# A new hand-written instruction order ahead of an expert loop, and row scalings moved to the end of the loop's first iteration

## The chip, the cores and the metric

One Trainium2 chip, one of its cores. A core has five engines that each run their own queue in order: PE (matmul; weight loads are listed as PEld), DVE (VectorE), ACT (ScalarE), POOL (GpSimd) and SP (SyncE, which here only issues DMAs). They wait for each other through semaphores alone. The metric is the device time in microseconds (us), the median of several executions.

## What is computed

The program is an attention step in both directions, and behind it a mixture of experts whose routing is balanced in eight rounds. The reference, cut to what matters:

```
# x: (8, 8, 512, 64)  batch, head, token, channel;  state: (8, 8, 32, 64)
scores = x @ state^T / 8 ;  a  = softmax(scores) ;  xread = a  @ state
scores2= state @ x^T / 8 ;  a2 = softmax(scores2);  sread = a2 @ x
X = concat([xread, sread], axis=2) -> (4352, 512)      # 8 x (512 + 32) rows

P = exp(X @ w_gate - max)                              # (4352, 8)
for _ in range(8):                                     # rows, then columns
    P /= P.sum(1) + 1e-9 ;  P /= P.sum(0) + 1e-9 ;  P *= N / E
out = sum over e of  P[:, e] * (relu(X @ w1[e]) @ w2[e])   # w1: 512x1024, w2: 1024x512
```

## The kernel before, in words

The 4352 rows are kept in nine blocks: eight of 512 rows, one for each batch (x's reads), and a ninth of 256 rows (the state's reads). `acc`, the output in fp32, stays in SBUF throughout.

**Ahead of the loop** lies everything up to the routing weights, interleaved with expert 0, so that PE has matmuls while the small work goes on. For each batch b (0 to 7) and half q of its heads: x is loaded by POOL's DMA queue (line 476, two halves a batch), turned either by PE (line 586, batches 0 and 1) or by a DMA transpose on SP's queue (line 599, into `xT`), scored against the state (line 613, one matmul group "S" for each half, numbered 0 to 15), brought through both softmaxes on DVE, ACT and POOL, and for the state's side turned by another DMA transpose on SP's queue (line 752, into `ETs`) for the matmuls that read x (line 775, "R"). Expert 0 needs for each block a projection "V" of w1 through the state (line 901), eight hidden matmul pairs "H" (line 928) with a relu each on ACT or DVE (lines 427, 429), and eight half sums "Y" of four matmuls (line 966). The balancing, on DVE, has eight rounds with one column sum on PE each (line 876). At the end expert 1's first block is begun.

**The order** of all this is written out by hand, as the table PLAN: 768 entries, each a number and an engine (P PE, V DVE, A ACT, G POOL, S SP's DMA queue, H nothing on the chip). An entry is one operation, one to sixty-four instructions. Each engine runs its entries in the table's order; semaphores wait for data and for buffers. PSUM buffers are taken in the table's order from a ring of six banks, so an entry that takes a bank waits until the entries that read the bank's previous content have run. The score banks (one pair) are handed on in the same way. x has five buffers, `xT` four. IDLE lists entries ahead of which PE gets so many dummy transposes.

Entries that are spoken of below:

| entries | what they are |
|---|---|
| 8, 9; 11, 12; 14, 15; 17, 18 | loads of x, first and second half, of batch 0; 1; 2; 3 |
| 24; 26; 29, 30 | loads of x: batch 5 second half; batch 6 first half; batch 7 |
| 51, 52; 53, 54 | loads of expert 0's w1 (two column halves) and w2 (two row halves) |
| 130, 131; 161; 192; 254 | DMA transposes of x: batch 2 both halves; batches 3, 4, 6 first half |
| 76, 91; 159; 190 | DMA transposes of the softmax of score groups 0, 1; 5; 7 |
| 132, 146, 177, 194 | score groups S4, S5, S7, S8 on PE |
| 315, 319, 321 | the matmuls that read x for batches 0, 2, 3 (R1, R5, R7) |
| 436, 470; 441; 479 | V's second half for blocks 0 and 1; first H of block 0; an early H of block 1 |
| 429; 430 to 432 | the last column sum on PE; DVE's three steps behind it |

**The loop** runs over the other experts e and blocks bi, 63 iterations (i). An iteration has seven parts k = 0 to 6. In each, `layer2` issues one of seven matrix products of eight matmuls on PE (line 341) into the banks A, E and Bseed, which DVE adds into `acc` with the routing weight (line 355), and `layer1` issues hidden matmuls of the next block (line 261) whose relu ACT does (line 284, `Hm`); after the fourth and eighth relu DVE makes four sums of them (lines 290 to 293). Two products that use the same bank wait for DVE's addition in between. While e is 1, the next block's four row tiles of `acc` have to be scaled by expert 0's routing weight first (`weigh`: line 303 on ACT, line 305 on DVE or POOL). In iteration 0 no projection falls due, so the parts in which the next block's scalings were issued are 0, 0, 1 and 2, on ACT, each ahead of the relus of its part.

Of the kernel before, what the change touches and what calls it, by code (L numbers as in the profile page):

```python
# [13 lines left out]
AF = mybir.ActivationFunctionType  # L14
EPS = 1e-9
PLAN = """
6G 0S 1S 2V 7H 44V 3A 33V 32A 34A 8G 56P 36P 35V 55H 37V 10H 45V 57A 42P 58V 9G 38P 40P 43A 59P 4S 39A 41V 5V
46V 62P 50H 51G 61A 71V 63P 60A 52G 64V 11G 72V 73A 78P 65V 12G 467P 433P 66A 79V 13H 14G 15G 53G 16H 80V 77P
47P 67V 468A 86V 68V 469A 434A 81A 470P 435A 48A 87V 93P 436P 471A 49A 92H 472A 69P 96P 82V 95V 88A 83V 94V
70V 437A 84P 99P 85V 89V 438A 107A 501P 74V 441P 75G 98V 439P 97V 54G 502A 453P 503A 442A 454A 445P 19H 129H  # L20
440A 100V 17G 443P 108V 101V 449P 447P 504P 102V 446A 114P 444A 451P 103A 109V 90V 450A 461P 336P 110A 115V
448V 116V 464P 130S 122A 354V 505A 506A 104V 160H 111V 132P 117G 452A 140V 458P 455P 118A 123V 462P 456P 459P
141V 18G 105G 337V 119V 76S 112G 106V 142A 465P 124V 133V 143V 134V 120G 91S 463A 125A 144G 131S 121V 146P
466V 113S 126V 457A 477P 135G 460A 479P 478A 147V 161S 154V 475P 487P 148V 136A 20G 155V 480A 21G 156A 145S
483P 137V 149G 473P 162S 485P 481P 163P 476A 488A 474A 150A 484V 315P 489P 486A 316A 191H 482V 495P 138G 127G
171V 164V 498P 128S 172V 22H 165V 173A 192S 166G 535P 167A 151V 177P 496P 152G 537A 497A 23G 222H 490P 139V
185V 499P 174V 186V 157V 158G 153V 187A 536V 509P 491A 317P 500A 168V 178V 318V 569P 179V 538P 510A 175G 169V
194P 539A 540A 202V 25H 570A 159S 571A 180G 195V 24G 492P 196V 517P 27G 197G 193S 493P 511P 519P 176S 181A
521P 203V 182V 513P 494A 188V 204A 507P 518A 520V 515P 512A 26G 514V 170V 508A 208P 198A 522A 216V 183G 209V
319P 184V 523P 516A 205V 526P 217V 199V 223S 524P 320A 210V 527P 218A 189G 200V 224S 547P 532P 225P 549P 219V  # L30
548A 211G 528V 529P 533P 525A 28H 233V 226V 234V 227V 530P 212A 29G 534A 543P 550V 213V 541P 551P 206V 545P
190S 542V 235A 214G 236V 531A 555P 553P 546V 544A 603P 207S 239P 552A 321P 253H 228G 240V 247V 556A 254S 554A
560P 255S 241V 248V 605A 220G 340P 604A 201V 563P 322A 229A 221S 561P 572P 242G 237G 249A 230V 256P 562A 250V
574A 231G 215V 341A 573A 564P 243A 557P 264V 257V 342P 558P 565A 265V 581P 266A 244V 31G 238S 258V 343V 577P
559A 637P 582A 578A 270P 566P 245V 338P 638A 284H 278V 567P 575P 259V 579P 271V 279V 639A 285S 251G 232V 272V
30G 273G 260A 261V 583P 339A 568A 589P 580V 280A 576A 587P 267V 323P 584A 606P 590A 588A 287P 246V 286S 344P
585P 324A 274A 607A 295V 608A 252S 275V 591P 586A 346P 296V 262V 288V 600P 615P 592P 281V 268G 297A 593A 601P
289V 263V 345V 602A 640P 301P 276G 616V 641A 269S 347V 642A 325P 290G 298V 326A 309V 282G 623P 597P 302V 299V
594P 291A 598P 310V 613P 303V 277V 617P 311A 283S 312V 313V 304G 300S 292V 614V 305A 293G 624A 306V 294V 595P
611P 619P 599A 348P 307G 308V 596A 618A 609P 331H 327P 314S 612A 349A 329P 620A 332G 621P 328V 610A 350P 330V  # L40
352P 351V 631P 334G 622A 651P 353V 652A 355V 356P 357V 632P 358P 625P 633A 359V 360A 727H 653P 626P 361V 362V
627A 335G 628P 363V 364V 365V 634P 366P 629P 367V 635P 655P 643P 368V 369V 654A 370V 630A 649P 636A 371V 645P
372V 656A 647P 657P 644A 373V 374V 375P 650V 737P 728H 376V 377V 333G 378V 646A 648A 658A 379V 380V 381V 738A
382V 671P 672A 383V 729V 662P 735G 665P 673A 739A 663P 730G 664A 666P 384P 674P 385V 386V 387V 740P 667A 659P
676A 388V 668P 675A 389V 679P 390V 660P 669P 741A 687P 391V 677P 680A 742A 392V 743H 670A 661V 393P 689P 748P
731G 755P 394V 678A 395V 396V 688A 397V 685P 690A 683P 756A 749A 686A 398V 759P 399V 691P 684A 400V 401V 681P
746P 757P 402P 682V 758V 760A 732V 403V 404V 405V 744P 745V 733G 406V 692A 407V 750P 747A 751A 753P 707P 705P
408V 409V 706A 693P 708A 410V 702P 699P 752V 754A 703P 411P 696P 412V 700P 694P 734G 695A 413V 414V 704V 697P
415V 711P 701A 709P 416V 417V 418V 419V 715P 420P 719P 698V 421V 712A 422V 423V 713P 716A 424V 425V 710A 714A
717P 426V 720A 724P 721P 718A 427V 428V 761V 725P 722P 429P 726A 430V 723A 762P 763A 431V 765P 432V 764A 766V  # L50
736G 767A
""".split()
ENGINES = {"P": "PE", "V": "DVE", "A": "ACT", "G": "POOL", "D": "DMA", "S": "SPQ", "H": "HOST"}
IDLE = {56: 50, 63: 3, 78: 3, 93: 8}
NT_ = 2
NE = 5
ETX = 0
# [13 lines left out]
PATV = (0, 0, 1, 3, 2, 2, 0)  # L71
# [37 lines left out]
def issue(ops, idle):  # L109
    for step in PLAN:  # L110
        op = ops[int(step[:-1])]
        assert all(d.end for d in op.after) and ENGINES[step[-1]] in op.on
        for slot in op.takes:
            slot.ring.taken.append(slot)
            slot.tile = slot.make()
        idle(op.takes[0].tile if op.takes else None, IDLE.get(int(step[:-1]), 0))
        op.emit(ENGINES[step[-1]])
# [5 lines left out]
def kernel(  # L123
# [19 lines left out]
    NTB = N // 128  # L143
# [11 lines left out]
    blocks = [(b * S, S) for b in range(B)] + [(NX, B * Ns)]  # L155
# [10 lines left out]
    def bank(shape, dtype, name, tag="bank"):  # L166
        return pools[tag].tile(shape, dtype, name=name, tag=tag)
# [26 lines left out]
    def load_w(e):  # L194

        w1h = mw.tile([128, NKC, F], FP16, name="w1h", tag="w1h")
        w2h = mw.tile([128, NFB, Dm], FP16, name="w2h", tag="w2h")
        w16[e] = (w1h, w2h)
        for g in range(2):
            nc.gpsimd.dma_start(out=w1h[:, ds(2 * g, 2), :], in_=w1r[e, :, ds(2 * g, 2), :])  # L200
        for g in range(2):
            nc.gpsimd.dma_start(out=w2h[:, ds(NJ * g, NJ), :], in_=w2r[e, :, ds(NJ * g, NJ), :])
        for _ in range(10):
            yield
        T = tpool[0].tile([128, 4, NJ, DH], FP16, name="T", tag="T")
        tsum[e] = T
        b11, b12 = w2h[:, :NJ, :DH], w2h[:, :NJ, DH:]
        b21, b22 = w2h[:, NJ:, :DH], w2h[:, NJ:, DH:]
        for i, (p, q) in enumerate(((b12, b11), (b22, T[:, 0]), (b22, b12), (b21, T[:, 1]))):
            for g in range(2):  # L210
                jj = ds(g * (NJ // 2), NJ // 2)
                nc.vector.tensor_sub(T[:, i, jj], p[:, jj], q[:, jj])
                yield
# [873 lines left out]
    for i, (e, bi) in enumerate(work):  # L1087
        if bi == 1 and e + 1 < E:
            wload.append(load_w(e + 1))
        if (e, bi) == final:  # L1090
            layer2_last()
            break
        v, pat = iter(()), PATS if bi == B else PATN if bi == B - 1 else PAT0
        soon = work[:i + (3 if bi == B - 1 else 2)]
        need = sum(b < B for _, b in soon) * (F // 512)
        if halves and all_halves - len(halves) < need:
            v, pat = project(halves[:SESSION], i), PATV
            del halves[:SESSION]
        if i:
            next(v, None)  # L1100
        if not i:
            seeds += [bank([128, 2, DH], FP32, "Bseed", "B%d" % k) for k in range(2)]
        l2 = layer2(e, bi, i)
        l1 = iter(())
        if i + 1 < len(work) and work[i + 1] not in hid:
            l1 = layer1(*work[i + 1], None if i else seeds[0].rearrange("p c d -> p (c d)"))
        if not i:
            next(l2)
            next(l1)
        for k in range(7):  # L1110
            next(l2)
            step(k)
            if k == 0:
                next(v, None)
                next(v, None)
            if late:
                late.pop()()
            for m in range(4) if e == 1 and bi < B else ():
                lead = pat is PATV and m == 0
                if k == ((0, 4, 5, 6) if pat is PATV else (0, 0, 1, 2))[m] and blocks[bi + 1][0] // 128 + m < NTB:  # L1120
                    weigh(blocks[bi + 1][0] // 128 + m, "DVE" if lead else "ACT")
            for _ in range(pat[k]):
                next(l1, None)
                step(k)
        for part in (l1, l2):
            for _ in part:
                pass
        if bi == len(blocks) - 3:
            for _ in (x for w in wload for x in w):
                pass  # L1130
            wload.clear()
# [30 lines left out]
```

## Time and profile before

| what | value |
|---|---|
| time before, median of 3 runs | 748.18 us (747.88 to 749.77) |
| the profiled execution's own time | 748.45 us |
| its span, first to last instruction | 746.7 us |
| PE / DVE / ACT / POOL busy | 99% / 82% / 69% / 11% of the span |
| first H of block 0 starts (PE, line 928) | 19.1 us |
| last column sum of the balancing (PE, line 876) | 130.5 us |
| the loop's first product (PE, line 341) | 131.2 us |

The profiled execution took 1.75 us more than its span, and 0.27 us more than the median. The span divides at 131.2 us: what lies ahead is the table's, what lies behind is the loop's.

### The profile page before, as it was taken

The numbers are of one execution on the slowest core, as the hardware profiler recorded it, in microseconds if no ns is written. First come the engines' busy times: TensorE is split into PE (matmuls) and PEld (weight loads), VectorE is DVE, ScalarE is ACT, GpSimd is POOL, SyncE is SP. The second block draws the span as 40 slices with busy tenths as digits, with TensorE's granted clock in tenths as the row PEclk, the third lists the DMA queues.
The fourth block names the chain that finished last, engine by engine and source line by source line (L and its number), as shares of the span: only waits on it lengthen the run. The fifth ranks groups of instructions, "written<-read, shape, count | busy, mean of one in ns | idle before, by whom it ended". The sixth has DMA issues, their size and how long they took to land.

```text
span 746.7 us, 16258 instructions
## 1 busy us (share of the span) xinstructions
PE 736.4 (99%) x6579; PEld 505.4 (68%) x6579; DVE 611.2 (82%) x1517; ACT 513.6 (69%) x1002; POOL 81.5 (11%) x97
## 2 busy tenths in 40 slices
PE   7999999999999999999999999999999999999997
PEld 6444545676777667776777767777777767776676
DVE  5989788788888788788888888887887888887885
ACT  6878764898876766767666666667666676667662
POOL 4775530200010000100000000100001000000000
PEclk9999999999999999999999999999999999999999
DMA  9997540600041000600005000330006000012233
GB/s 178 175 159 92 86 79 1 114 1 2 1 85 29 2 1 1 113 2 1 1 16 99 1 1 2 66 48 1 2 1 113 1 2 1 1 39 94 97 113 142
DMA packets 51371, 36.71 MB, mean 49 GB/s; under 512 B 25312, under 2 KB 44000, under 8 KB 51296
## 3 DMA queue, kind: packets, MB, share of 16 engines
q0 software_dynamic: 22272, 20.97, 18.3%
q1 hardware_dynamic: 27840, 14.31, 8.0%
q8 instruction: 51, 0.84, 0.4%
q10 hardware_dynamic: 1184, 0.39, 0.2%
q14 instruction: 24, 0.20, 0.1%
HBM read 42.48 MB, written 8.91 MB: 69 GB/s over the span
## 4 chain that ended last, share of the span: by engine, by line
PE 93%; DMA 2%; ACT 2%; POOL 1%; DVE 1%; issue 1%; SPq 0%; POOLq 0%; ACTq 0%
PE hps L261 28%; PE Bseed L341 20%; PE A L341 14%; PE E L341 14%; PE yps L966 6%; PE hps L928 4%; PE v_ps L241 4%; DMA x_nat<-in_x_dram 1%; DMA xT<-x_nat 1%; PE v_ps L901 1%; PE su_ps L775 0%; PE y L320 0%; ACT acc L303 0%; ACT hT L427 0%; POOL x_nat L476 0%
## 5 line engine op out<-in xcount | busy, mean ns | idle before, releaser
L284 ACT ACTIVATE Hm<-hps 128x512 f16<-128x512 f32 (+1 forms) x495 | 264.6, 576 | 130.7 <-PE hps L261 128.9
L341 PEld LDWEIGHTS <-Hm 128*128 128x128 f16 x1888 | 181.7, 98 | 72.0 <-issue 16.3
L261 PE MATMUL hps<-aT,V 128*128 128x512 f16 x878 | 230.1, 379 | 0.0
L355 DVE SCALAR_TENSOR_TENSOR acc<-Bseed,Pmat,acc 128x256 f32<-128x256 f32 x354 | 155.0, 478 | 9.3 <-PE Bseed L341 6.4
L341 PEld LDWEIGHTS <-sm 128*128 128x128 f16 x1416 | 138.3, 98 | 34.5 <-issue 0.3
L341 PE MATMUL Bseed<-T,Hm 128*128 128x256 f16 x944 | 123.3, 273 | 0.7 <-DVE acc L355 0.7
L341 PE MATMUL A<-w2h,Hm 128*128 128x256 f16 x944 | 123.7, 273 | 0.0
L261 PEld LDWEIGHTS <-V 128*128 128x128 f16 x880 | 86.1, 98 | 50.7 <-ACT V L421 0.2
L355 DVE SCALAR_TENSOR_TENSOR acc<-E,Pmat,acc 128x256 f32<-128x256 f32 x236 | 103.2, 477 | 12.1 <-PE E L341 12.0
L290 DVE TENSOR_TENSOR sm<-Hm 128x512 f16<-128x512 f16 (+1 forms) x122 | 50.3, 412 | 61.1 <-ACT Hm L284 61.1
L249 ACT CAST V<-v_ps 128x512 f16<-128x512 f32 x144 | 74.2, 610 | 0.0
L355 DVE SCALAR_TENSOR_TENSOR acc<-A,Pmat,acc 128x256 f32<-128x256 f32 x118 | 51.9, 480 | 17.2 <-PE A L341 17.1
L966 PE MATMUL yps<-w2h,hT 128*128 128x512 f16 x272 | 64.0, 379 | 0.3 <-ACT hT L427 0.3
L341 PE MATMUL E<-T,sm 128*128 128x256 f16 x472 | 61.7, 273 | 0.1
L341 PE MATMUL E<-w2h,sm 128*128 128x256 f16 x472 | 61.7, 273 | 0.0
L341 PE MATMUL Bseed<-T,sm 128*128 128x256 f16 x472 | 61.6, 272 | 0.0
L365 ACT COPY Bseed<-A 128x512 f32<-128x512 f32 (+1 forms) x62 | 34.1, 550 | 37.6 <-PE A L341 35.1
L291 DVE TENSOR_TENSOR Hm<-Hm 128x512 f16<-128x512 f16 (+1 forms) x122 | 50.2, 412 | 4.2
L293 DVE TENSOR_TENSOR sm<-Hm,sm 128x512 f16<-128x512 f16 (+1 forms) x122 | 50.2, 412 | 4.2
L200 POOL DMA_DIRECT2D w1h<-in_moe_w_dram x12 | 8.6, 717 | 397.0 <-PE hps L261 396.6
L292 DVE TENSOR_TENSOR sm<-sm,Hm 128x512 f16<-128x512 f16 (+1 forms) x122 | 49.4, 405 | 0.0
L966 PEld LDWEIGHTS <-hT 128*128 128x128 f16 x272 | 25.2, 98 | 29.4 <-issue 1.6
(133 smaller groups left out, 621.2 us busy)
## 6 DMA issues: line engine op xcount, KB each, us to landing
out_dram<-acc SPq DMA_DIRECT2D x33, 256.0 KB, 2.6
w1h<-in_moe_w_dram POOLq DMA_DIRECT2D x16, 512.0 KB, 7.0
w2h<-in_moe_w_dram POOLq DMA_DIRECT2D x16, 512.0 KB, 7.5
x_nat<-in_x_dram POOLq DMA_DIRECT2D x16, 256.0 KB, 5.9
st_st<-in_state_dram SPq DMA_DIRECT2D x1, 256.0 KB, 3.9
st_st<-in_state_dram ACTq DMA_DIRECT2D x1, 256.0 KB, 4.5
ETs<-E SPq DMA_TRANSPOSE x16, 3.5
xT<-x_nat SPq DMA_TRANSPOSE x12, 4.3
```

The lines of the kernel that those rows point to most:

```text
L241: nc.tensor.matmul(ps[q][ds(j * Ns, Ns), :], stT[ds(r, 64), bi, q, ds((j ^ q) * Ns, Ns)], w1h[ds(r, 64), 2 * q + j // 2, cols], tile_posit ...
L249: nc.scalar.copy(out=dst, in_=src)
L261: nc.tensor.matmul(out, lhs, rhs, start=(k == 0), stop=(k == len(terms) - 1))
L284: nc.scalar.activation(out=Hm[:, i, j, :tn], in_=hps[:, :tn], func=AF.Relu)
L290: nc.vector.tensor_add(s1, a21, a22)
L291: nc.vector.tensor_sub(a21, a11, a21)
L292: nc.vector.tensor_sub(s2, s1, a11)
L293: nc.vector.tensor_sub(s4, a12, s2)
L341: nc.tensor.matmul(dst[:, c], lhs(j, c), rhs[:, j], start=first and c == 0 and j == 0, stop=(j == NJ - 1), skip_group_check=True)
L355: nc.vector.scalar_tensor_tensor(out=dst, in0=src[:, c], scalar=p[:, k], in1=dst, op0=ALU.mult, op1=ALU.add)
L365: nc.scalar.copy(out=Bb[:, :nk], in_=A[:, :nk])
L966: nc.tensor.matmul(yps.tile, hT[fb].tile[:, ds(tk * 128, 128)], w2h[:, fb, :], start=(fb == 0), stop=(fb == NFB - 1))
```

## The change

The table is replaced by another order of the same 768 entries, some of them on another engine: DVE has 248 entries where it had 241, ACT 186 where it had 185, POOL 58 where it had 66, PE and SP as many as before. IDLE names other entries: 3 dummies ahead of entry 62 and 12 ahead of 436, in place of 3 ahead of 63 and 8 ahead of 93. In the loop, iteration 0 issues the next block's four scalings in its parts 3, 4, 5 and 6, still on ACT and still ahead of the part's relus; the other iterations keep their parts. The diff, with the table cut:

```diff
--- before.py
+++ after.py
@@ -14,44 +14,43 @@
 PLAN = """
-6G 0S 1S 2V 7H 44V 3A 33V 32A 34A 8G 56P 36P 35V 55H 37V 10H 45V 57A 42P 58V 9G 38P 40P 43A 59P 4S 39A 41V 5V
-46V 62P 50H 51G 61A 71V 63P 60A 52G 64V 11G 72V 73A 78P 65V 12G 467P 433P 66A 79V 13H 14G 15G 53G 16H 80V 77P
-47P 67V 468A 86V 68V 469A 434A 81A 470P 435A 48A 87V 93P 436P 471A 49A 92H 472A 69P 96P 82V 95V 88A 83V 94V
-70V 437A 84P 99P 85V 89V 438A 107A 501P 74V 441P 75G 98V 439P 97V 54G 502A 453P 503A 442A 454A 445P 19H 129H
-440A 100V 17G 443P 108V 101V 449P 447P 504P 102V 446A 114P 444A 451P 103A 109V 90V 450A 461P 336P 110A 115V
-448V 116V 464P 130S 122A 354V 505A 506A 104V 160H 111V 132P 117G 452A 140V 458P 455P 118A 123V 462P 456P 459P
-141V 18G 105G 337V 119V 76S 112G 106V 142A 465P 124V 133V 143V 134V 120G 91S 463A 125A 144G 131S 121V 146P
...
-415V 711P 701A 709P 416V 417V 418V 419V 715P 420P 719P 698V 421V 712A 422V 423V 713P 716A 424V 425V 710A 714A
-717P 426V 720A 724P 721P 718A 427V 428V 761V 725P 722P 429P 726A 430V 723A 762P 763A 431V 765P 432V 764A 766V
-736G 767A
+6G 0S 1S 2V 7H 44V 3A 33V 32A 34A 8G 56P 36P 35V 55H 37V 10H 45V 57A 42P 58V 9G 38P 43A 39V 40P 46A 41A 4S 59P
+61A 5V 62P 60A 71V 63P 50H 78P 51G 64V 13H 72V 11G 467P 65V 79V 433P 73A 52G 80V 12G 66A 77P 468A 435A 67V 14G
+53G 47P 54G 86V 49V 434A 469A 81A 436P 87V 470P 68V 129H 48V 88A 437A 69P 16H 438A 471A 472A 93P 82V 96P 83V
+92H 70A 94V 84P 501P 98A 95V 99P 85V 100V 441P 89V 97A 107A 503A 445P 101V 502V 442V 439P 15G 446A 443P 114P
+115V 102G 444A 451P 130S 17G 108V 447P 109V 453P 440A 160H 103A 449P 116V 122A 90V 19H 18G 74V 123V 448A 452A
+131S 161S 110A 104V 117G 461P 454A 111V 450A 105G 112G 455P 75V 458P 118A 124V 504P 132P 462P 506A 140V 133V
+119V 141V 463A 125A 459P 336P 134V 120G 106V 142A 121V 505A 143V 456P 337V 464P 457A 146P 465P 76S 460A 135G
...
+167A 496P 186V 491V 168V 222H 187A 191H 178V 500A 159S 317P 153V 497A 188V 192S 319P 569P 179V 320A 169G 180G
...
+27G 176S 219V 527P 205V 226V 524P 543P 234V 227V 254S 531A 534V 212A 206G 547P 554A 528V 213V 548V 235A 228G
...
+545P 220G 201V 525A 229A 544A 549P 546A 541P 214G 555P 284H 542V 342P 550A 556A 572P 230V 190S 574A 603P 239P
...
+247V 248V 343A 573A 231G 321P 604A 240V 551P 241V 249A 552V 605V 560P 236V 557P 256P 340P 250V 561P 338P 341V
...
+749V 403V 729V 404V 405V 730V 756A 406V 717P 759P 407V 709P 753P 696P 408V 409V 718A 702P 410V 760A 731V 699P
+411P 710A 700P 412V 693P 701A 703P 697P 413V 754A 414V 705P 415V 416V 417V 418V 694P 735G 419V 698A 420P 695A
+704V 707P 761V 711P 744P 706A 708A 719P 712A 750P 421V 422V 713P 736G 715P 423V 424V 425V 426V 427V 745A 720A
+714A 724P 716A 428V 751V 721P 752V 725P 429P 726A 722P 430V 762P 431V 432V 723A 732V 764V 765P 763A 766A 767A
 """.split()
-IDLE = {56: 50, 63: 3, 78: 3, 93: 8}
+IDLE = {56: 50, 62: 3, 78: 3, 436: 12}
@@ -1116,8 +1115,8 @@
             if late:
                 late.pop()()
             for m in range(4) if e == 1 and bi < B else ():
-                lead = pat is PATV and m == 0
-                if k == ((0, 4, 5, 6) if pat is PATV else (0, 0, 1, 2))[m] and blocks[bi + 1][0] // 128 + m < NTB:
+                lead = i and pat is PATV and m == 0
+                if k == ((3, 4, 5, 6) if not i else (0, 4, 5, 6) if pat is PATV else (0, 0, 1, 2))[m] and blocks[bi + 1][0] // 128 + m < NTB:
                     weigh(blocks[bi + 1][0] // 128 + m, "DVE" if lead else "ACT")
             for _ in range(pat[k]):
                 next(l1, None)
```

POOL's queue begins 8 9 51 **52 11** 12 14 **15 53** 75 **54** 17 18 before, and 8 9 51 **11 52** 12 14 **53 54 15** 102 17 18 after (75 and 102 are arithmetic on POOL that waits for DVE). SP's queue begins 130 76 91 131 113 161 145 162 before and 130 131 161 76 91 162 113 128 145 159 192 after; later it has 224 176 254 190 where it had 176 223 224 190 207 254.

More of the change, by code (lines that the diff above doesn't have):

```diff
@@ L22 @@
-448V 116V 464P 130S 122A 354V 505A 506A 104V 160H 111V 132P 117G 452A 140V 458P 455P 118A 123V 462P 456P 459P
-141V 18G 105G 337V 119V 76S 112G 106V 142A 465P 124V 133V 143V 134V 120G 91S 463A 125A 144G 131S 121V 146P
-466V 113S 126V 457A 477P 135G 460A 479P 478A 147V 161S 154V 475P 487P 148V 136A 20G 155V 480A 21G 156A 145S
-483P 137V 149G 473P 162S 485P 481P 163P 476A 488A 474A 150A 484V 315P 489P 486A 316A 191H 482V 495P 138G 127G
-171V 164V 498P 128S 172V 22H 165V 173A 192S 166G 535P 167A 151V 177P 496P 152G 537A 497A 23G 222H 490P 139V
@@ L27 @@
[L27 to L46, printed above, removed]
@@ L47 @@
-746P 757P 402P 682V 758V 760A 732V 403V 404V 405V 744P 745V 733G 406V 692A 407V 750P 747A 751A 753P 707P 705P
-408V 409V 706A 693P 708A 410V 702P 699P 752V 754A 703P 411P 696P 412V 700P 694P 734G 695A 413V 414V 704V 697P
-415V 711P 701A 709P 416V 417V 418V 419V 715P 420P 719P 698V 421V 712A 422V 423V 713P 716A 424V 425V 710A 714A
-717P 426V 720A 724P 721P 718A 427V 428V 761V 725P 722P 429P 726A 430V 723A 762P 763A 431V 765P 432V 764A 766V
-736G 767A
+6G 0S 1S 2V 7H 44V 3A 33V 32A 34A 8G 56P 36P 35V 55H 37V 10H 45V 57A 42P 58V 9G 38P 43A 39V 40P 46A 41A 4S 59P
@@ new lines @@
+119V 141V 463A 125A 459P 336P 134V 120G 106V 142A 121V 505A 143V 456P 337V 464P 457A 146P 465P 76S 460A 135G
+479P 20G 475P 126V 136A 91S 473P 480A 147V 487P 477P 466A 154V 148V 483P 144V 149G 474A 162S 155V 476V 156A
+481P 113S 485P 137V 482V 21G 127V 478A 315P 128S 138V 157V 488A 535P 484A 163P 145S 498P 150A 489P 536A 171V
+164V 316A 172V 486A 22H 165V 158G 495P 538P 173A 151V 166G 177P 490P 139V 539A 499P 540A 537V 185V 23G 152G
+167A 496P 186V 491V 168V 222H 187A 191H 178V 500A 159S 317P 153V 497A 188V 192S 319P 569P 179V 320A 169G 180G
@@ new lines @@
+31G 28H 194P 492P 511P 202V 24G 318A 571A 195V 509P 29G 193S 513P 174V 493P 570A 203V 223S 25H 512A 517P 196V
+181A 510A 519P 182V 494A 204A 514A 521P 197G 224S 507P 183V 508A 518V 170V 30G 198A 26G 520A 515P 208P 216V
+253H 529P 522A 532P 217V 523P 175V 209V 199V 210V 184V 189V 526P 218A 516A 225P 233V 200G 533P 211V 530P 553P
+27G 176S 219V 527P 205V 226V 524P 543P 234V 227V 254S 531A 534V 212A 206G 547P 554A 528V 213V 548V 235A 228G
+545P 220G 201V 525A 229A 544A 549P 546A 541P 214G 555P 284H 542V 342P 550A 556A 572P 230V 190S 574A 603P 239P
@@ new lines @@
+247V 248V 343A 573A 231G 321P 604A 240V 551P 241V 249A 552V 605V 560P 236V 557P 256P 340P 250V 561P 338P 341V
+215V 257V 322A 558P 237V 258V 285S 563P 559V 242G 243A 264V 566P 221S 562A 255S 259G 564P 232V 579P 265V 260A
+261V 244V 266A 567P 267V 339A 251V 637P 580A 270P 286S 344P 245G 565A 262G 639V 568A 575P 278V 246V 581P 331H
+638A 345V 207S 577P 576A 589P 587P 268G 271V 582A 585P 279V 583P 578A 272V 590A 588V 252S 346P 273G 323P 280A
+586A 606P 281V 324A 287P 584V 600P 347A 591P 274A 601P 607A 275V 295V 288V 296V 238S 608A 335G 297A 282G 609P
@@ new lines @@
+592P 602A 640P 301P 276V 289V 325P 642A 593A 290G 298V 309V 594P 597P 310V 610A 302V 299G 595P 291A 311A 303V
+641A 277V 283S 613P 304G 312V 263V 326A 313V 305A 292V 596A 598P 354V 306V 619P 307V 599A 620A 623P 617P 308V
+293G 611P 334G 269S 614A 348P 294V 624A 615P 621P 618A 300S 327P 314S 349V 616A 329P 612A 350P 328V 330A 631P
+351A 622V 352P 353V 355V 632P 633A 356P 357V 625P 358P 634P 359V 360A 628P 361V 362V 727H 647P 363V 635P 333G
+364V 626P 636A 365V 366P 367V 368V 627A 369V 370V 629P 728H 655P 651P 648A 332G 371V 645P 630A 656A 653P 372V
@@ new lines @@
+649P 657P 373V 374V 652A 654A 643P 646A 650A 375P 644A 658V 737P 738A 376V 671P 377V 665P 378V 662P 379V 673A
+380V 381V 666P 739A 663P 382V 383V 733V 384P 385V 386V 672A 740P 734V 667A 664A 674P 741A 675A 387V 668P 388V
+659P 389V 742A 743H 390V 391V 676A 392V 669P 679P 670A 660P 393P 680V 394V 395V 757P 661A 677P 685P 396V 746P
+686A 758V 397V 678A 689P 747A 398V 399V 683P 684A 691P 681P 690A 682A 687P 400V 748P 401V 688A 402P 692V 755P
+749V 403V 729V 404V 405V 730V 756A 406V 717P 759P 407V 709P 753P 696P 408V 409V 718A 702P 410V 760A 731V 699P
```

## The prediction

> **What bounds the kernel now.** I read the page first, then PE by windows, then PE's list of waits, then the chain of work that ended last.
>
> ```profile
> span 746.7 us, 16258 instructions
> ...
> PE 736.4 (99%) x6579; PEld 505.4 (68%) x6579; DVE 611.2 (82%) x1517; ACT 513.6 (69%) x1002; POOL 81.5 (11%) x97
> ```
>
> PE is busy 99% of the span, so a reordering can win back only PE's idle time and what hides inside "busy" (slow clock, late starts). The windows show where that is (columns: busy us and count for each engine, PE's granted clock, DMA share, GB/s):
>
> ```profile
> 10.00:20.00 10.00, 7.61 (x167) 4.57 (x165) 8.98 (x23) 7.94 (x20) 0.82 (x1) 0.83 1.34 199
> 20.00:30.00 10.00, 10.00 (x75) 4.34 (x74) 9.43 (x25) 9.45 (x21) 6.68 (x9) 1.00 1.35 188
> 30.00:40.00 10.00, 9.14 (x98) 4.00 (x96) 8.62 (x20) 7.47 (x17) 8.77 (x10) 1.00 1.21 169
> ...
> 140.00:150.00 10.00, 9.28 (x89) 6.29 (x88) 8.11 (x21) 7.38 (x14) 0.00 (x0) 1.00 0.75 126
> ```
>
> PE misses 2.4 us between 10 and 20, 0.9 between 30 and 40, 0.7 behind 140, and almost nothing elsewhere. Who ends those waits:
>
> ```profile
> PE xT_ps L586 <- DMA x_nat<-in_x_dram: 1.3, 2, 0.7
> PE Bseed L341 <- DVE acc L355: 0.7, 1, 0.7
> PE G_ps L528 <- ACT V L421: 0.7, 1, 0.7
> PE psB L613 <- DMA xT<-x_nat: 0.5, 1, 0.5
> ```
>
> Loads and DMA transposes end the early ones; the one behind 140 is DVE's. For the table I use one measure, PE's **lag**: an entry's start minus PE's issue time for all entries listed ahead of it (from the starts: hidden pair 0.43 us, half sum 0.865, projection or score 0.225, R 0.62, turn of x 0.5). A reordering that makes PE wait less has a smaller lag at the loop. Before, the lag is 12.7 us at 441 (starts 19.14), 13.0 at 132 (25.31), 13.2 at score S6, 14.45 at 177 (39.59), 14.6 at S9, 15.0 at S14, 15.6 at S15 (80.15) and 16.5 at the loop. Much of the slow growth is a change of matmul shape (309 ns where 216 is usual), which no order removes.
>
> **The change part by part.** Times below are places in the profiled execution; a minus is a gain.
>
> *(a) Start, to the first H.* The loads land at 10.7 (51), 13.7 (52), 15.4 (11), 16.7 (12): one after another, an x half in 1.3 to 1.7 us, a w half in 2.6 to 2.95. With 11 ahead of 52, 11 lands near 12.3 and 52 near 15.2. PE now waits at 436 for 52, where it waited for 11 at 15.43. The groups behind the wait are nearly the same ones, but x's turn need not wait any more. Then ACT decides: its evictions from 437 on start at 15.65 and follow each 0.48 us (steps 20.28, 20.77, 21.27 in its timeline), so 441 has its inputs at 18.3 to 18.8 in place of 19.14, and 454 and 450, which free 504's bank and feed the second half sums, end at 24.8 and 25.3. 132 then starts near 25.1 with 13.0 us of work ahead of it, where it was 25.31 with 12.35: 0.85. I take **-0.6** (-1.0 to 0).
>
> *(b) S5.* Load 15 now stands behind both halves of w2. From 14's landing at 18.0 the rows give 20.65 (53), 23.4 (54), 24.7 (15). 131 issues at 24.8 (before 23.84) and lands 4.1 to 5.1 later (161 and 130 took that) at 28.9 to 29.9. S5 is due at 16.9 + 12.2 = 29.1. I take **+0.4**. Ends: 0, and 3.5 if 54 takes its old 4.7 us from 53's landing and 131 its own 5.96. Behind S5 wait DVE's three entries on it, and the relus behind those.
>
> *(c) The two waits between 34 and 40* (0.3 on a relu, 0.55 on 162's transpose; lag 13.2 to 14.45). After, SP has 131, 161, 76, 91, 162 in a row, 1.2 to 1.5 us each: 162 issues at about 30.5, in place of 33.62, and lands by 36.4 even with its 5.92. S7 is due at 25.4 + 12.9 = 38.3. **-1.1** (-1.2 to 0).
>
> *(d) R5 and S8.* R5 comes 5.9 us of PE work earlier. Its transpose 159 follows DVE's and POOL's work on group 5 (done near 37.2), issues at 38 and lands 3.3 to 4.3 later, at 41.3 to 42.3; R5 is due at 41.8. 192 issues behind it, lands at 42.3 to 43.1; S8 is due at 42.7. **+0.1** (0 to 1.5).
>
> *(e) R7.* 190 now stands on SP behind 254, and 254 waits for load 26. POOL reaches 26 behind 197, 30 at about 49.1; it took 5.9 to land: 55.0. Then 254 occupies SP for 1.25 and 190, issued at 56.3, lands 3.7 later: 60.0. R7 is due at 46.4 + 13.4 = 59.8. **+0.5**; ends 0 and 4.0 (26 like 27's 6.2, 190 like 285's 7.2).
>
> *(f) S15's wait* (0.3 idle for ACT's `acc` at 79.7, lag 15.0 to 15.6): its bank changes hands elsewhere now. **-0.25** (-0.5 to 0).
>
> *(g) DVE.* From 441 to 270 (S13) the table now lists 49.4 us of DVE work (steps of its timeline, summed) beside 49.2 of PE work; it was 46.1 beside 47.7. DVE waited about 4 us in that stretch before. Some relus and copies that free PE's banks will come late. No row shows which: **+0.4** (0 to 2, half of DVE's old waits).
>
> *(h) The balancing and the table's end.* Four subtractions for T move from POOL to DVE (0.43 each on DVE). On POOL they slowed DVE:
>
> ```profile
> 105.56 1.44 DVE L869 SCALAR_TENSOR_TENSOR Pmat<-crec,Pmat 128x272 f32<-128x272 f32 x1
> ```
>
> The same step takes 0.44 otherwise. PE did not wait for it, so this wins nothing. A round is 3.45 us on DVE from one column sum to the next, PE's work between two is 4.0 to 5.7, and what DVE gets besides fits, but for four relus and sums behind the sixth to eighth round that use up the slack. 429 comes one half sum earlier, DVE ends its part about as long ahead of the loop's first use as before (PE lost 0.2 there at 132.3). **0** (-0.2 to +0.4).
>
> *(i) Iteration 0.* The chain:
>
> ```profile
> 133.86 2.56 ACT acc L303 x4
> ...
> 137.51 0.98 ACT Hm L284 x2
> ...
> 138.52 0.44 DVE sm L290
> ...
> 140.20 0.80 DVE acc L355 x2
> ...
> 141.04 1.03 PE Bseed L341 x8
> ```
>
> Four scalings at once (one is layer2's own) hold ACT, so the fourth relu ends at 138.5, DVE's sums start late, its additions stand behind them, and PE's last product waits (0.72 idle, 0.89 over its pace). Moved to parts 3 to 6, three of the four no longer stand ahead of that relu: it ends near 137.4, the sums by 139.1, the addition by 139.9, and PE is due at 140.15. The price: 4 x 0.64 to 0.71 us later on ACT, among relus that come every 0.87 us from PE, and in ACT's idle 1.5 us ahead of 142.47. The last scaling ends at 141.7, and its row is first added to at 143.9. If the cover failed, the casts behind 142.5 would be late by up to 0.7. **-0.8** (-0.9 to 0).
>
> **Sum:** -0.6 + 0.4 - 1.1 + 0.1 + 0.5 - 0.25 + 0.4 + 0 - 0.8 = -1.35. On the profiled execution's 748.45 that is 747.1; it lay 0.27 over the median, so I predict **746.8**. A measurement of this kernel can tell about 0.3% (2.24 us) from no change: 745.9 and 750.4 are the bounds.
>
> **The rivals.**
>
> *No transfer is late* (b, d, e and g cost nothing): -0.6 - 1.1 - 0.25 - 0.8 = -2.75, 745.4. For it: each of the margins in (b), (d), (e) is within 1 us of zero, so small luck clears them. Against: transposes took 2.4 to 7.2 us, and six entries depend on it.
>
> *The waits only change place* (the reorder does not do what it says): (b), (d), (e) cost 1.0 more together and (c)'s gain shrinks to half, +1.5: 748.3. For it: DMA engines are full to 45 us (share 1.2 to 1.35), so what one transfer gains another loses.
>
> *Slower: R7's transpose.* 190 behind 254 behind load 26, all in SP's order. From a landing at 61.7 on this alone takes back the gain, from 63.9 on the whole is over 750.4. At 64, the worst rows, it costs 4.0, 3.5 above the forecast; the late R7 also holds its bank and so half sums on ACT: 750.5. For it: 285, issued likewise amid x loads, took 7.2. Against: most transposes there took 3.3 to 4.5.
>
> *The clock.* In the start the clock was halved:
>
> ```profile
> 16.00:17.00 1.00, 1.00 (x14) 0.56 (x14) 0.91 (x2) 1.00 (x4) 0.00 (x0) 0.51 1.43 193
> ...
> 19.00:20.00 1.00, 1.00 (x12) 0.40 (x5) 1.00 (x4) 1.00 (x3) 0.82 (x1) 0.78 1.18 195
> ```
>
> It came behind PE's thin stretch from 11 to 16, and a 128-column turn took 107 ns in place of 56 until 19.4. If PE's longer wait at 436 leads to a second such stretch of 3.4 us, in the H pairs, PE loses half of it, 1.7: 748.5. If it never comes, ACT's evictions still hold 441 to 18.3, which lies in (a). The Trainium skill, "TensorE: Matmul & The Clock Gate", section "What's actually happening", says that the half rate is the default, that activity releases it, and that this is judged in free-running windows of some 3.4 us. This trace's stretch of half rate agrees in length; by that rule which window is judged idle can differ from run to run.
>
> **How the numbers follow.** Forecast, 745.9 to 748.2: 0.41. No transfer late: 0.26. Waits change place: 0.13. Slower: 0.12. Clock: 0.08. Faster by over 0.3%: most of the second case and a little of the first, 0.25; slower: 0.13; the same: 0.62. The range 744.6 to 749.6 leaves out most of the slower case and the best ends of (a), (f) and (i) together.
>
> **What would show it.** In the profile after: 441 at 18.3 to 18.8; a granted clock of 0.5 for 3.4 us at most; PE's wait on `xT` gone from S7 and at most 0.8 at S5; R5, S8 and R7 with under 1 us of waits; a lag at the loop of 15.2 to 16.3; no wait of PE's Bseed on `acc` in iteration 0, and from its end on the same pace to the same tail. Wrong it would be by a transpose or load over 6 us at S5, R5 or R7, by DVE as PE's releaser between 45 and 90, or by PE's Bseed still waiting in iteration 0.

## The result, and the profile after

The changed kernel takes **753.16 us** (median of 6, 752.26 to 754.94), the kernel before 748.4 (now the median of 6, 747.88 to 749.77): a ratio of 1.0053, with a 95% interval of 1.0032 to 1.0075. The forecast was 746.8, in a range of 744.6 to 749.6. The change made the kernel slower by 4.8 us, and the forecast had the other sign.

The profiled execution has a span of 751.1 us, 4.4 more than before. The page shows where it is not: PE's busy time grew by only 1.8 us, so most of the loss is idle time.

```profile
span 751.1 us, 16257 instructions
...
PE 738.2 (98%) x6583; PEld 506.6 (67%) x6583; DVE 613.1 (82%) x1524; ACT 514.5 (69%) x1003; POOL 72.1 (10%) x89
```

The windows say when (columns as before: busy us and count of PE, PEld, DVE, ACT and POOL, PE's granted clock, DMA share, GB/s):

```profile
30.00:40.00 10.00, 10.00 (x110) 4.50 (x110) 9.80 (x25) 8.71 (x20) 6.14 (x8) 1.00 1.14 161
40.00:42.00 2.00, 2.00 (x30) 0.95 (x30) 1.97 (x5) 1.53 (x5) 1.00 (x1) 1.00 0.64 52
42.00:44.00 2.00, 1.17 (x61) 0.84 (x54) 1.97 (x6) 1.90 (x6) 1.05 (x1) 1.00 1.31 190
44.00:46.00 2.00, 0.00 (x0) 0.00 (x0) 0.12 (x1) 0.51 (x2) 1.66 (x4) 0.70 1.36 90
46.00:47.00 1.00, 0.53 (x9) 0.28 (x10) 0.05 (x1) 0.00 (x0) 1.00 (x2) 0.50 1.29 252
...
50.00:51.00 1.00, 1.00 (x3) 0.30 (x2) 0.26 (x1) 1.00 (x3) 1.00 (x3) 0.50 1.24 167
```

Between 30 and 40 PE misses nothing now, where it missed 0.9: that step of the forecast holds. But from 43.2 on PE stands for 3.3 us, and when it goes on its clock is at 0.5, until 51.6: "busy" is 1.00, with three matmuls in the microsecond, 427 ns each where 216 is usual. The list of PE's waits and the chain name the releaser:

```profile
PE psB L612 <- DMA xT<-x_nat: 4.1, 2, 3.3
...
PE mT_ps L834 <- DVE lmx L831: 0.4, 1, 0.4
```

```profile
39.26 7.07 DMA xT<-x_nat
46.33 0.14 issue
46.47 0.41 PE psB L612 x8
```

It is score S8, waiting for its transpose 192: issued at 39.26, landed at 46.33, 7.07 us, where it took 3.14 before. (The kernel's lines are one less than before's: L612 is the score, L613 before.) PE's **lag** (its start minus the issue time of all that is listed ahead), the measure of the forecast, shows what this cost. It is 13.35 at S7 (14.44 before), 16.82 at S8, 19.36 at S9 behind the stretch of half clock, and 21.64 at the loop (16.48 before). In the loop 0.76 came back: from the loop's first product to the end of the span 614.68, before 615.44.

### The profile page after: what moved, and what is told of

Its sections match the earlier page's. It is cut to its first block, busy times and chain, and to the rows that moved or that the text cites. A ratio compares the mean times of both kernels' runs of the same rounds, so it can differ in the third digit from the quotient of the medians.

```text
span 751.1 us, 16257 instructions
## 1 busy us (share of the span) xinstructions
PE 738.2 (98%) x6583; PEld 506.6 (67%) x6583; DVE 613.1 (82%) x1524; ACT 514.5 (69%) x1003; POOL 72.1 (10%) x89
## 4 chain that ended last, share of the span: by engine, by line
PE 94%; DMA 4%; POOL 1%; ACT 1%; DVE 0%; issue 0%; POOLq 0%; DVEq 0%; SPq 0%
PE hps L260 28%; PE Bseed L340 21%; PE A L340 14%; PE E L340 14%; PE yps L965 7%; PE hps L927 4%; PE v_ps L240 4%; DMA xT<-x_nat 2%; DMA x_nat<-in_x_dram 2%; PE y L319 0%; POOL x_nat L475 0%; PE su_ps L774 0%; PE v_ps L900 0%; PE psB L612 0%; ACT hT L426 0%
## 5 line engine op out<-in xcount | busy, mean ns | idle before, releaser
L340 PEld LDWEIGHTS <-Hm 128*128 128x128 f16 x1888 | 181.7, 98 | 71.0 <-issue 15.3
L354 DVE SCALAR_TENSOR_TENSOR acc<-A,Pmat,acc 128x256 f32<-128x256 f32 x118 | 51.9, 479 | 16.8 <-PE A L340 16.7
```

Source lines behind the costliest of these rows:

```text
L340: nc.tensor.matmul(dst[:, c], lhs(j, c), rhs[:, j], start=first and c == 0 and j == 0, stop=(j == NJ - 1), skip_group_check=True)
L354: nc.vector.scalar_tensor_tensor(out=dst, in0=src[:, c], scalar=p[:, k], in1=dst, op0=ALU.mult, op1=ALU.add)
```

## The experiments

**Theories.** The timeline shows what was issued at the same moment:

```profile
39.12 0.80 POOL L475 DMA_DIRECT2D x_nat<-in_x_dram  x1
39.26 1.28 SPq L598 DMA_TRANSPOSE xT<-x_nat  x1
```

*A*: the load 23, issued on POOL 0.14 us ahead of 192, takes the DMA engines from it. Before, 192 went out 1.6 us ahead of that load, and took 3.1:

```profile
38.02 1.25 SPq L599 DMA_TRANSPOSE xT<-x_nat  x1
...
39.65 0.81 POOL L476 DMA_DIRECT2D x_nat<-in_x_dram  x1
...
DMA to landing us min/median/max: 3.1/3.1/3.1
```

*B*: 192 is late because on SP it now stands behind 159, where it stood ahead of it. *C*, seen in the second experiment: a fetch of instructions holds the transposes up as well. The kernel before ran beside each group. Of the experiments that change the table, only entries named in the diff are moved.

**1. The loop's part alone.** Before's table, with the scalings of iteration 0 in parts 3 to 6.

```diff
-lead = pat is PATV and m == 0
-if k == ((0, 4, 5, 6) if pat is PATV else (0, 0, 1, 2))[m] and ...
+lead = i and pat is PATV and m == 0
+if k == ((3, 4, 5, 6) if not i else (0, 4, 5, 6) if pat is PATV else (0, 0, 1, 2))[m] and ...
```

> Before's table and IDLE, with the change's new parts for the four scalings of iteration 0 alone. If step (i) is right and stands by itself, PE's product of iteration 0 no longer waits for DVE (0.72 idle, 0.89 over its pace in before), what lies behind the first entry of the loop is 0.75 shorter than in before (614.99 us from that entry to the span's end in the changed kernel, 615.75 in before), and the run takes 747.6 where before takes 748.4. Rival: the shorter loop of the changed kernel comes from the state in which its table hands over (buffers free earlier); then this run shows 615.75 again and the wait on acc.

Measured: 747.83 beside 748.99, ratio 0.9997 (0.9969 to 1.0026), so the time itself decides nothing. The trace does: from the loop's first product to the end 614.55 in place of 615.44, and PE's list of waits has no `acc` from line 355 any more. Step (i) holds, by itself, at 0.9.

**2. Load 23 later.** (222 takes a buffer for the data of 23, and goes with it.)

```diff
-185V 23G 152G
+185V 152G
...
-168V 222H 187A
+168V 187A
...
-320A 169G 180G
+320A 169G 23G 222H 180G
```

> The changed kernel with x's load 23 issued behind POOL's step 169 (at about 43.5 in place of 39.1 us); SP's order is kept. Theory A (transposes share the DMA engines with the load): the transpose 192, issued at 39.3, has the engines to itself and lands at 42 to 42.8 in place of 46.3; S8's wait of 3.3 falls under 0.3, no stretch of half clock follows, the lag at the loop is 15.6 to 16.0 in place of 21.6, and the time is 747.2 (745.9 to 748.5). Theory B (192 is late because it is issued 1.2 us later than before, behind transpose 159 in SP's queue): it still lands after 45, S8 waits 2 us or more, time 751 to 753.

Measured: 751.49 beside 748.99, ratio 1.0030 (1.0015 to 1.0045). The time is one that B had given, the landing is between the two: 192 landed at 44.26. S8 lost 1.42 and no half clock followed. S10 lost 1.63: its transpose 223 now waited for load 23 and flew, from 47.9 to 55.3, beside four other loads. So A is about half of it. The rest showed in the DMA queues: no load ran beside 192, and yet its packets all but stopped from 42.7 to 43.7, just behind the start of a single packet of 16 KB of instructions (42.18 us, 0.88 long). Theory C is from here.

**3. 192 ahead of 159**, as before has them.

```diff
-159S 317P
+192S 159S 317P
...
-188V 192S 319P
+188V 319P
```

> The changed kernel with the transposes 192 (for S8) and 159 (for R5) in the other order on SP, as before has them; load 23 stays at 39.1 us. Theory B: S8's wait goes and R5 loses at most 1, so 747 to 748. Theory A: the load meets whichever transpose is issued second, so 192 (issued at 38.0) lands at 41 to 42, 159 (issued at 39.2) lands at 44 to 46, R5, due at 42.2, waits 2 to 4 us in place of S8, a half-clock stretch follows again, and the time is 751 to 753.

Measured: 753.12 beside 748.99, ratio 1.0051 (1.0035 to 1.0067). 192 landed 3.1 us after its issue; 159, now second and issued just after the load, took 6.9, and R5 (line 773 in this run) waited in S8's place, with a half clock of 3.41 us behind it:

```profile
PE su_ps L773 <- DMA ETs<-E: 3.9, 1, 3.9
```

B falls: whichever of the two is issued at the load's side is late, and the time is nearly the same.

**4. Dummies while PE waits for S8.**

```diff
-IDLE = {56: 50, 62: 3, 78: 3, 436: 12}
+IDLE = {56: 50, 62: 3, 78: 3, 436: 12, 194: 60}
```

> The changed kernel with 60 dummy transposes on PE ahead of S8 (3.4 us at full clock), so that PE is not idle while it waits for the transpose. If the half-rate stretch from 45 to 51.5 follows from PE's idleness, it does not come: PE's lag grows by 2.3 to 2.6 less behind S8, and the time is 750.6 (749.9 to 751.5). If it comes from something else (the load on the chip at that time, a fixed window), the granted clock still shows 0.5 behind S8, and the time is 753 to 754.

Measured: 751.18 beside 748.99, ratio 1.0031 (1.0018 to 1.0044); 192 took 7.2 and S8 came 3.6 late as before, but the clock stayed up:

```profile
46.00:48.00 2.00, 2.00 (x33) 1.42 (x30) 0.52 (x1) 0.00 (x0) 1.80 (x4) 1.00 0.61 72
```

The lag was 17.46 at S8 and 17.53 at S9. The time is inside the forecast of 749.9 to 751.5. The half clock behind S8, worth 2.54 us in the changed kernel's profile, follows from PE's idleness and not from the late transfer as such.

**5 and 6. Fewer dummies ahead of S8**, so that PE's fetch comes later; in 6 load 23 also behind 152 (and 222 behind 191).

```diff
-IDLE = {56: 50, 62: 3, 78: 3, 436: 12}
+IDLE = {56: 20, 62: 3, 78: 3, 436: 5}
...
-23G 152G
+152G 23G
```

> The changed kernel with 37 dummy transposes fewer on PE ahead of S8 (20 in place of 50 at the start, 5 in place of 12 ahead of 436), so that PE reaches its next block of instructions some 3 us of work later, behind S8. Theory C: the 16 KB fetch of PE's instructions (44.16 us in the changed kernel, 42.18 in the one with load 23 later) stops the transposes for 1.5 to 2 us, on top of the load's share. Then no 16 KB fetch lies between 39 and 46, 192 (issued at 39.3) lands at 44.3 to 45.0, S8 waits 1.3 to 2.0 in place of 3.3, and the time is 749 to 751.5 (less if no half-clock stretch follows). Rival: the silent 1.5 us are the load's doing alone; 192 then lands at 46.3 again and the time is 752 to 754. The start may lose up to 0.5 by the missing dummies.

> The changed kernel with the same 37 dummies fewer, and load 23 issued behind step 152 (about 41.0 in place of 39.1). If load and fetch together are the whole cause, 192 lands at 42 to 43, S8 waits under 0.3, no half-clock stretch follows, S10 does not wait either (23 lands near 45.5 and its transpose 223 by 50), the lag at the loop is 15.4 to 16.2, and the time is 747.2 (746.2 to 748.2). If there is a third cause, 192 lands after 44 and the time is 749 or more.

Measured: 753.71 and 752.86 beside 749.0, ratios 1.0055 (1.0039 to 1.0070) and 1.0046 (1.0027 to 1.0065). Both expectations missed. With 30 dummies fewer at the start PE stood 3.2 and 3.5 us for the first load, 441 came at 19.6 and 20.1 (18.2 in the changed kernel), and the transposes moved back with it: in 5 the fetch (44.85) met 192 again (6.2 from issue to landing), which settles nothing. In 6 the fetch came at 47.0, behind 192's landing, but 192 (issued at 40.84) met the load (41.07) and took 5.7: load without fetch.

**7. Load 23 earlier, in the kernel before.**

```diff
-173A 192S 166G
+173A 192S 23G 166G
...
-497A 23G 222H
+497A 222H
```

> The kernel before with load 23 moved ahead of POOL's step 166, so that it is issued at about 37.7 in place of 39.7, with transpose 192 at 38.0 as before. Theory A: 192 lands at 42.5 to 44.5 in place of 41.2 though its own place is unchanged. Theory B: it lands at 41.2 as before. S8 is due at 44.0, so the time moves by less than 1 us in either case; the landing decides.

Measured: 748.74 (one run) beside 749.0. 192 took 4.26 in place of 3.14 and landed at 42.60 in place of 41.16, though nothing of its own was moved: A, in the other kernel and the other direction.

**8. w2's second half later.**

```diff
-53G 47P 54G 86V
+53G 47P 86V
...
-115V 102G 444A
+115V 102G 54G 444A
```

> The changed kernel with the load 54 of w2's second half issued behind POOL's step 102 (about 20.9 in place of 7.6), so that 130's transpose (17.7) runs beside fewer loads. Theory A: 15 lands by 23, 130 lands at 23 to 24 in place of 25.9 and S4's wait of 0.8 goes; but 54 lands near 27, and the second half sums (first one due at 25.4) wait about 1 us instead: no gain, the lag at S5 13.0 to 13.6. Rival: 130 is late for another reason and S4 waits again.

Measured: 758.64 (one run). Transpose 130 took 5.0 in place of 8.2 and landed at 23.0, so S4 waited no more, as A says. But 54 landed only at 29.95, the half sum 462 waited 3.3 us for it, and S8 3.6 more for its transpose (7.2, with load 23 and a fetch in its flight). I had put that price at 1 us.

**9 and 10. The loads apart, without and with the fetch apart.** Both have load 23 behind 169, as in 2, and 29 and 30 behind 27 and 206; 10 also has 12 dummies fewer.

```diff
-195V 509P 29G 193S
+195V 509P 193S
...
-170V 30G 198A
+170V 198A
...
-27G 176S
+27G 29G 176S
...
-206G 547P
+206G 30G 547P
...
-IDLE = {56: 50, 62: 3, 78: 3, 436: 12}
+IDLE = {56: 44, 62: 3, 78: 3, 436: 6}
```

> The changed kernel with load 23 behind step 169 (43.5 us, as in the second experiment) and the loads 29 and 30 moved behind steps 27 and 206 (54 to 57 us in place of 46.6 and 50.1), so that transpose 223 too meets fewer loads. Theory A: 223 lands by 52.5 and S10 waits under 0.3, where the second experiment lost 1.6. The 16 KB fetch still falls in 192's flight (42.2): by theory C S8 waits 1.2 to 1.6 again. Lag at the loop 16.9 to 17.4, time 748.3 to 749.5. If the loads are all of it, S8 waits under 0.3 and the time is 747.

> The same, with 12 dummies fewer (44 at the start, 6 ahead of 436), so that PE's fetch comes about 1 us later, at 43.2, when 192's packets are through. Theory C: 192 lands at 42.3 to 43.2, S8 waits under 0.3, the lag at the loop is 15.4 to 16.2, and the time is 747.2 (746.4 to 748.2). Without theory C: S8 waits 1.2 to 1.6 as before, 748.3 to 749.5.

Measured: 751.13 and 750.16 beside 749.89, ratios 1.0013 (0.9995 to 1.0031) and 1.0004 (0.9990 to 1.0018). In 9 the fetch fell at 41.88, 192 took 4.6 and S8 lost 1.16. In 10 it fell at 43.66, 192 took 3.3, landed at 42.85, and S8 lost nothing: lag 13.50, after 13.52 at R5. The times stayed over the forecasts: S10 still lost 0.9 and 1.9, since 223, issued at 48.0, met the loads 24 and 26 and landed near 54.4; and the kernel before itself took 749.89 beside them, 1.5 more than in the first measurement.

The four cells, from issue to landing of 192:

| | no fetch in its flight | a fetch in its flight |
|---|---|---|
| no load beside it | 3.3 (run 10), 3.1 (before) | 4.6 (run 9), 4.9 (run 2) |
| load 23 beside it | 5.7 (run 6) | 7.1 (changed kernel), 7.2 (runs 4 and 8), 6.2 (run 5, its load 1.9 us ahead) |

Each is one profiled execution. Where load 23 had been issued 1.4 to 2.3 us ahead, it met 192 only in part, and 192 took 4.3, 4.8 and 4.2 (runs 7, 11 and 12; in 12 a fetch began 0.13 us ahead of the landing). Transpose 193 follows 192 by 1.3 us in run 10 as in the changed kernel, so it is not the cause.

The queues show load and fetch at work (queue, kind, packets, MB, share of 16 engines; q0 carries POOL's loads, q1 SP's transposes). The changed kernel from 42 to 43, load and transposes together:

```profile
q0 software_dynamic: 228, 0.12, 85.7%
q1 hardware_dynamic: 231, 0.06, 44.8%
```

Run 10 from 41 to 42, transposes alone:

```profile
q1 hardware_dynamic: 958, 0.24, 118.4%
```

The changed kernel from 44.5 to 45.5, behind a 16 KB fetch at 44.16 and with no load left:

```profile
q1 hardware_dynamic: 71, 0.02, 84.4%
```

In the first of these microseconds one transpose packet passes for each load packet, 231 for 228, where 958 pass alone. Behind the fetch it is 71. The Trainium skill, "DMA: Bandwidth & Descriptors", section "Queues, rings and completion order", says that each DMA engine takes turns between its queues packet by packet; the 228 to 231 agrees. Other microseconds have other mixtures (before, 36 to 37: 329 load packets and 164 of transposes), so one for one is not shown as a rule.

The fetch's part does not hang on the four cells alone. In the packet records of all 14 traces, between 15 and 95 us, a transpose in flight for over 2 us all but stood still 44 times: for 0.75 to 1.75 us, fewer than 12 transpose packets and fewer than 8 of loads passed in each quarter of a microsecond. Every time this began within 1.2 us of the start of an instruction fetch of 8 or 16 KB, and such surroundings cover only a sixth of the time. The kernel before has it too, behind fetches at 31.19, 66.46 and 77.58.

**11 and 12. Load 23 two microseconds earlier in the changed kernel**, ahead of 166; 11 also with the 12 dummies fewer.

```diff
-151V 166G
+151V 23G 166G
...
-23G 152G
+152G
...
-IDLE = {56: 50, 62: 3, 78: 3, 436: 12}
+IDLE = {56: 44, 62: 3, 78: 3, 436: 6}
```

> The changed kernel with load 23 ahead of POOL's step 166 (issued at about 37.1 in place of 39.1, so that it is through before 192's packets) and the 12 dummies fewer that put PE's fetch behind 192. By theories A and C 192 lands at 42.5 to 43.6, S8 waits under 0.5, transpose 223 goes out at 42 to 44 ahead of the loads 24 and 29 as in the changed kernel and lands by 48, so S10 does not wait either; 159 may come up to 0.5 late for R5. Lag at the loop 16.0 to 16.8, time 747.0 to 748.0 where before takes 748.4 to 749. If the load and the fetch are not the cause, S8 waits 1 us or more and the time is 750 or more.

> The same with the changed kernel's own dummies, so that the fetch is back at 41.5 to 42.5, in 192's flight. By theory C 192 lands at 44 to 45, S8 waits 1 to 2 us, time 1 to 3 us over that of the run beside it. If the fetch does not matter here, the two agree within 0.5 us behind S8.

Measured: 749.10 and 749.91 beside 749.57, ratios 0.9994 (0.9985 to 1.0003) and 1.0008 (0.9990 to 1.0025). Both times are over the forecast for 11 (747.0 to 748.0). Run 12 differs from the changed kernel in the place of one load, and its profiled span is 746.7 in place of 751.1: 192 took 4.2, S8 lost nothing, no half clock, lag at the loop 17.26 in place of 21.64. That profiled execution is the fastest of its ten (748.45; the slowest took 753.08), so the medians gain less, 753.16 to 749.91. Its fetch fell at 43.47, as 192 landed, since PE had waited 1.1 for an earlier transpose (R1), so it does not test C. In 11, 192 took 4.8 beside the load's end and R5 and S8 lost 1.4 together; the start was at half clock for 6.8 us, and the lag at the loop was 17.66, over my 16.0 to 16.8. No version here is faster than the kernel before by more than its interval.

## Why the prediction was wrong, point by point

Differences of PE's lag, after against before, in the profiled executions:

| step | forecast | measured | |
|---|---|---|---|
| (a) start, to S4 | -0.6 | 0.0 | 441 0.96 earlier, then S4 waits 0.8 for 130 |
| (b) S5 | +0.4 | -0.02 | 131 landed at 29.8, S5 at 30.0 |
| (c) waits at 34 to 40 | -1.1 | -1.07 | right |
| (d) R5 and S8 | +0.1 | **+5.85** | S8's wait, and the half clock behind it |
| (e) R7 | +0.5 | 0.0 | PE itself came 4.9 late; in run 12, 0.2 |
| (f) S15 | -0.25 | -0.47 | the wait for `acc` is gone |
| (g) DVE | +0.4 | +0.43 | 0.35 of it at 356, PE waiting for `lmx` |
| (h) balancing | 0 | +0.44 | PE waits for ACT at 106 |
| (i) iteration 0 | -0.8 | -0.76 | right; by itself 0.9 (run 1) |

All but (d) add up to -1.45, and the forecast's to -1.45. That they agree is in good part chance, since (a), (b), (e) and (h) missed by 0.4 to 0.6 each, and the misses cancel. The sign was decided by **(d)**, which had read "192 issues behind it, lands at 42.3 to 43.1", with a worst case of 1.5. Two things failed in that step.

*The duration.* I gave 159 the 3.3 to 4.3 us that neighbouring transposes had taken and let 192 land 0.8 to 1.0 us behind it, which is 3.0 to 3.8 us from its issue at 39.3; it took 7.07. I treated the duration as if it belonged to the kind of instruction. Here it depends on what flies beside it: by run 6 the load alone makes it 5.7, and the 1.3 us left fall, by difference, to the fetch, which the forecast had no term for. The trace of before showed the load's part, sorted that way: with no packets of a load beside them, 192, 254, 255 and 286 took 3.1 to 3.4; beside loads, 130, 131, 161, 162, 193, 223, 224 and 285 took 3.8 to 7.2 (some of these with a fetch in flight too). I quoted "2.4 to 7.2" for all of them and used it as luck. The diff moved load 23 from 1.6 us behind 192 to 0.14 ahead of it, and I never looked for that load's new place: I followed SP's queue, and POOL's only for the loads that S5 and R7 need themselves. The same oversight is in (a): 130 took 8.2 in place of 5.1, because 15 and 54 now fly until 25.3, and took 5.0 with 54 out of the way (run 8).

*What a wait costs.* The clock rival named the mechanism, at another place: a second half-rate stretch behind entry 436, 1.7 us. It came behind S8's 3.3 us, lasted 6.8, and cost 2.54 on top of the wait. Run 4 shows it is the idleness: with PE kept busy it did not come. Waits of 1.2 (run 2) and 1.7 (run 10, for S10) brought none, waits of 2.6 and 3.9 (runs 6 and 3) a stretch of 3.41 us each.

Of the rivals, the slower one had the right kind of cause, one transpose behind loads, but at R7, and so at 750.5. "The waits only change place" named (d), and gave it with two others 1.0 together.

The signs named S5, R5 and R7 as places of a transpose over 6 us, and not S8. Of the other signs I had listed, 441 came at 18.18, just ahead of 18.3 to 18.8; in the runs 2 and 9, with the same table up to there, at 18.95 and 19.08. The difference is the half-rate stretch at the start: none in this execution, one of 3.41 us from 15.3 and 15.75 in those. The kernel before had one too, and 441 at 19.14. So of (a)'s 0.96 at 441 only 0.1 to 0.2 is left where both have a stretch: the gain was, for the most part, luck with that stretch and not the order of the loads. By the rule of "TensorE: Matmul & The Clock Gate" in the Trainium skill, section "What's actually happening", that the windows run free of the kernel, such a difference between executions is expected; the stretches here, 3.41 and 6.83 us, agree with its window.

The 0.44 of (h) is a wait that the forecast put at nothing. The chain of the changed kernel shows it, at a projection of w1 (line 900) that waits for ACT's relus; the lag grows by 0.6 there:

```profile
104.14 2.07 ACT hT L426 x4
106.21 0.04 issue
106.26 0.41 PE v_ps L900 x7
```

What stays open: (h) was not tried by itself. How one fetch packet can stop the transposes, no run shows; that it does is read from the 44 cases and from runs 9 and 10, which differ in 12 dummies and so in the start as well. Why single executions of run 12 took up to 753.08 is not shown either, since one was profiled.

## What to carry to other kernels

When a table or queue order moves a load, list every transfer that is in flight with it at its new time, on the other queues too, and give each the duration that rows with the same company have, not the mean of its kind. Waits of PE of 2.6 to 3.9 us cost another 1.6 to 2.5 in clock here (the changed kernel, runs 3 and 6), so price the clock behind a long wait as well, or fill the wait with dummies (run 4). Give the due time of a transfer that feeds PE the worst duration of its company: here a load that moved from 1.6 us behind a transpose to 0.14 ahead of it started a loss of 5.9.

## What was not expected of the hardware

A transpose beside a load ran, in the microsecond shown, at a quarter of its rate (231 packets against 958); a load's packet is the larger there (512 bytes against 256) and the longer (60 ns against 31, from the shares). A 16 KB fetch of instructions, taken for PE's because it moves with PE's dummies, itself 0.9 to 1.3 us long in the kernels before and after, all but stopped the transposes for 0.75 to 1.75 us (71 packets in the microsecond shown) and cost 192 some 1.3 to 1.8 us. The Trainium skill, "Runtime: NRT & Kernel Launch", section "Instruction fetch mechanics", has the 16 KiB blocks on a queue of their own and calls their cost mostly hidden; for PE that holds here as far as its lists of waits show, which name no fetch, and for the transposes beside it not. Where PE's block ends is thus part of the timing: taking 12 dummies away moved the fetch from 41.9 to 43.7 and took 1.2 us from S8.
